# A new hand-run order for a fused cross attention and mixture-of-experts kernel: other places, PSUM banks and copying engines for the same steps

## The chip, the cores and the metric

The kernel runs on one core of one Trainium2 chip. Its engines are TensorE (PE in the profile; PEld is its loading of weights), VectorE (DVE), ScalarE (ACT), GpSimd (POOL) and SyncE (SP). The metric is device time in microseconds. The kernel before takes 209.95 us, the median of three runs from 209.51 to 209.97.

## The reference

Cross attention between 512 tokens and 32 states in each of 8 batches and 8 heads of width 64, both ways round, and then a two-layer network over all rows that come out. In float32:

```
scores  = x @ state.T / 8                       # per batch and head: 512 x 32
xread   = softmax(scores,   over the states) @ state      # 512 x 64
sread   = softmax(scores.T, over the tokens) @ x          # 32 x 64
rows    = concat(xread, sread), heads side by side        # 8 * 544 = 4352 rows of 512
h       = rows @ w_in                                     # 4352 x 2048
g       = max(h, 0) + alpha * min(h, 0)                   # alpha: one number per column
out     = g @ w_out                                       # 4352 x 512
```

Sums of softmax have 1e-9 added, which the kernel leaves out.

## The kernel before, in words

**Arithmetic.** All operands of matmuls are f16, all sums are f32. Since xread = a @ state, h of a batch is a @ (state @ w_in): the kernel makes m = state @ w_in for a batch (L486, 64-deep matmuls; it is copied from PSUM by L508), and then h for each of 16 blocks of 128 hidden columns (jc) as two 512-wide matmuls of m with the transposed attention weights aT (L519). The state reads of all batches are gathered in a tile XS (copied by L472) and go through w_in by themselves as a ninth "batch" of 256 rows (L528). g is made in two steps: ACT writes neg = relu(-h) (L551) and DVE writes gp = neg * (1 - alpha) + h (L569).

**The second layer.** Batch 0 takes plain products of gp with w_out (L588, called o, copied out by L761). Batches 1 to 7 and the reads take a scheme of seven products on 2x2 blocks instead of eight. It needs block sums of gp (s, numbered 1 to 4; L645 on POOL, or L621: a DMA from gp to gp that adds, issued by POOL) and sums of blocks of w_out (ws, L616, once). The products p (L668) add up in three PSUM chains per batch. From these, copies p1, p5 and u are taken (L699), c21 is a copy (L703), and c11, c12 and c22 are additions on DVE (L706). Each of the four c blocks is stored by SP (L579) or, near the end, by ACT (L582). For batch 7 the block c11 is made in three last pieces by L717 and L728.

**The attention of one batch.** Scores (sc, L326, 16 small matmuls) need x transposed (xT): for batches 0 and 1 by PE, for batches 2 to 7 by a DMA that transposes, issued by SP (L304), from the loaded x (xg, L175, issued by POOL, which casts to f16). For the softmax over the states DVE transposes 32x32 blocks of the scores (ts, L357) and takes maxima (mx, L365), POOL subtracts (L371), ACT takes exponentials (L377), DVE sums and inverts (L381, L382), POOL scales (an, L387), DVE transposes back (aT, L397). For the softmax over the tokens DVE takes maxima (nb, L409), ACT takes exponentials with sums (e, L424), e is scaled on ACT (L440) or POOL (L442), and a second transposing DMA on SP makes e2T (L446), from which PE makes the state reads (sr_ps, L461).

**What sets the order.** Nothing is planned by the compiler. One string, ORDER (from L17 on), lists some 1,180 tokens, and the program walks through it; each token calls one step, and the steps' instructions stand in each engine's own queue in just that order. An engine takes its next instruction only when the one before has been issued and its own waits are over. The numbers behind a token are batch, block and PSUM bank (k0 to k5 are single banks, and there is one double tile for scores and m); a letter names the engine that copies (a for ACT, v for DVE, p for POOL; d stands for the adding DMA). So `F.1.7.0` is h of batch 1, block 7, in bank 0; `N` and `G` are the neg and gp of a block; `S` and `P` are products; `A.1.1.0.d` is block sum 1 of half 0 of batch 1 by DMA; `sc`, `xd`, `tt`, `lx`, `m`, `mo`, `rd` and `rdo` are scores, transposing of x, transposing of e, load of x, m, the copy of m, the state reads and their copy; `T` is a weight sum, `Q` a block of the result, `W` a store, `Z` a number of matmuls on zeros (L245), which write to a bank that nobody reads.

**Buffers** that tie places in the list together: 2 for xT, 4 for xg, 2 for e2T, 5 for results to be stored (osb; p1, p5, u and the c blocks share them), 4 for neg, 2 for gp, 3 for each half's block sums. SP's queue holds, in one order, the six transposes of x, the eight of e and nearly all stores. POOL's queue holds the loads of x, w_in and w_out and the adding DMAs between its own sums.

Of the kernel before, what the change touches and what calls it, by code (L numbers as in the profile page):

```python
# [23 lines left out]
f.0.0.0.5 mo.0.0.a.1 xo.1.1.1.v xt.1.0.1.3 wo.2 f.0.2.0.4 tsum.0 m.1.1 wb.0.1 mo.3.0.a.0 xo.1.0.1.v
m.0.1.0.2 mo.1.1.v.0 tn.0.0 mo.0.1.v.0 f.0.2.1 f.0.0.1 mo.1.1.a.1 mo.0.1.a.1 f.0.1.0.1 f.0.1.1
F.0.3.3 m.4.0 N.0.0 N.0.1 F.0.5.2 N.0.2 F.0.4.0 G.0.0 G.0.1 N.0.3 G.0.2 F.0.7.5 N.0.5 N.0.4 G.0.3
S.0.1.0.1 mo.4.0.a.0 S.0.0.0.4 mo.4.0.a.1 G.0.4 S.0.0.1 S.0.1.1 lx.2 N.0.7 m.0.2.3.0 sc.1 G.0.5
mo.0.2.a.0 S.0.2.0.2 wo.3 G.0.7 m.1.2.5.3 mo.0.2.a.1 mo.1.2.a.0 S.0.2.1 sb.1 F.0.6.0 xd.2 mo.1.2.a.1
F.0.8.5 N.0.6 F.0.9.3 tm.1 S.0.1.2 N.0.8 S.0.2.2 S.0.0.2 G.0.6 S.0.1.3 te.1.1 te.1.0 N.0.9 F.0.11.0
smax.1 N.0.11 S.0.2.3 m.0.3 G.0.8 F.0.10.5 tn.0.1 T.0.0.p T.0.1.p S.0.0.3 mo.0.3.a.0 G.0.9 N.0.10  # L30
G.0.11 ssh.p.1 T.2.0.p S.0.3.0.3 mo.0.3.v.1 S.0.3.1 F.0.13.0 S.0.3.2 sexp.1 N.0.13 G.0.10 S.0.3.3
m.1.3 ssum.1 G.0.13 F.0.14.5 S.0.2.4 snorm.p.1 T.1.0.p N.0.14 G.0.14 S.0.1.4 wb.1 tt.0 F.0.12.0
N.0.12 G.0.12 S.0.0.4 F.0.15.5 S.0.3.4 mo.1.3.a.1 N.0.15 tsum.1 tn.1.0 S.0.1.5 G.0.15 S.0.0.5
S.0.2.5 mo.1.3.a.0 m.2.1 tn.1.1.a F.1.7.0 mo.2.1.v.0 S.0.2.6 N.1.7 mo.2.1.v.1 F.1.3.5 lx.3 tt.1
G.1.7 sc.2 S.0.2.7 tx.2 T.1.1.p F.1.9.0 O.0.2.a S.0.0.6 N.1.3 S.0.1.6 sb.2 N.1.9 S.0.0.7 ty.2
# [5 lines left out]
wb.2 W.O.0.0 P.1.1.3 N.1.15 m.2.2 N.1.13 P.1.2.1 A.1.3.1.p G.1.15 mo.2.2.a.1 F.1.14.0 mo.2.2.a.0
G.1.12 F.2.13.2 N.1.14 G.1.13 m.3.2 N.2.13 F.2.12.1 G.1.14 A.1.1.0.d mo.3.2.a.1 F.2.0.3 N.2.12
P.1.2.2 G.2.13 A.1.2.0.p F.2.9.0 N.2.0 G.2.12 P.1.2.3 N.2.9 F.2.8.2 G.2.0 Q.1.p1.a F.2.4.1
mo.3.2.a.0 tsum.2 G.2.9 A.1.1.1.d F.2.2.3 N.2.4 P.1.6.0 Q.1.c11.v W.Q.1.c11 xd.4 A.1.2.1.p tn.2.1.a
F.2.11.0 G.2.4 sc.3 N.2.11 P.1.6.1 tx.3 N.2.2 F.2.10.4 P.1.5.0.1 T.3.1.p N.2.10 G.2.11 P.1.6.2 ty.3
N.2.8 P.1.5.1 G.2.2 P.1.6.3 tn.2.0.a F.2.5.0 sb.3 Q.1.u.a tt.2 F.2.1.3 lx.5 P.1.5.2 G.2.8 P.1.7.0
te.3.0 A.1.4.0.p P.1.5.3 smax.3 te.3.1 P.1.7.1 F.2.3.2 N.2.5 G.2.10 P.1.7.2 Q.1.p5.a ssh.p.3 m.3.3
N.2.1 G.2.5 P.1.7.3 mo.3.3.a.1 G.2.1 P.1.3.0 N.2.3 F.2.15.4 tsum.3 Q.1.c22.v mo.3.3.a.0 P.1.3.1
A.1.4.1.p N.2.15 P.2.1.0.0 G.2.3 sexp.3 F.2.6.3 G.2.15 sc.4 P.1.4.0 tn.3.0.a tx.4 P.2.2.0.2
A.2.3.0.p F.2.7.4 ssum.3 P.2.2.1 ty.4 N.2.7 P.1.4.1 N.2.6 P.1.3.2 te.4.0 P.2.1.1 G.2.6 snorm.p.3  # L50
P.1.4.2 te.4.1 G.2.7 P.2.1.2 tn.3.1.a P.1.3.3 sb.4 F.2.14.3 tt.3 A.2.2.0.p P.1.4.3 N.2.14 tsum.4
P.2.1.3 Q.1.c12.v Q.1.c21.a rd.2.4 wb.3 W.Q.1.c22 Q.2.p1.a m.3.1 W.Q.1.c21 rdo.2.a m.5.1.1.5
A.2.1.0.d mo.3.1.a.0 P.2.2.2 G.2.14 xd.5 P.2.6.0 mo.5.1.a.0 A.2.3.1.p smax.4 F.3.10.4 mo.3.1.a.1
P.2.2.3 mo.5.1.a.1 F.3.13.3 N.3.10 Q.2.c11.v m.4.3 N.3.13 G.3.10 F.3.7.1 A.2.2.1.p P.2.6.1 W.Q.2.c11
N.3.7 G.3.13 F.3.2.5 mo.4.3.a.0 W.Q.1.c12 F.3.0.2 G.3.7 N.3.2 F.3.8.4 N.3.0 F.3.1.3 G.3.2 A.2.1.1.d
F.3.3.1 N.3.1 G.3.0 ssh.p.4 P.2.6.2 N.3.3 F.3.5.5 G.3.1 N.3.8 P.2.5.0.2 G.3.3 mo.4.3.a.1 P.2.6.3
N.3.5 lx.6 rd.3.3 Q.2.u.v sexp.4 m.4.2 G.3.5 A.2.4.0.p F.3.14.1 rdo.3.a G.3.8 P.2.5.1 mo.4.2.a.1
P.2.7.0 ssum.4 N.3.14 F.3.4.5 F.3.15.3 N.3.4 P.2.7.1 N.3.15 G.3.14 P.2.5.2 snorm.p.4 mo.4.2.a.0
P.2.7.2 G.3.4 P.2.5.3 G.3.15 sc.5 Q.2.p5.a m.4.1.4.1 tx.5 P.2.7.3 lx.7 mo.4.1.a.0 F.3.6.5 mo.4.1.a.1
F.3.12.3 A.2.4.1.p Q.2.c22.v N.3.6 P.2.3.0 ty.5 wb.4 N.3.12 F.3.11.1 P.2.4.0 te.5.0 F.3.9.4 G.3.6  # L60
N.3.11 P.2.3.1 A.3.3.0.p N.3.9 P.2.4.1 G.3.12 xd.6 F.4.0.5 G.3.11 P.2.4.2 N.4.0 F.4.7.3 sb.5
A.3.3.1.p P.2.4.3 N.4.7 P.3.1.0.1 Q.2.c21.a G.4.0 P.2.3.2 tn.4.0.a P.3.1.1 G.3.9 F.4.3.0 te.5.1
G.4.7 P.2.3.3 A.3.1.0.d N.4.3 P.3.1.2 tsum.5 A.3.1.1.d tn.4.1.a G.4.3 m.5.0 m.5.2.5.4 A.3.2.0.p
mo.5.0.a.0 P.3.1.3 mo.5.2.v.1 mo.5.2.a.0 F.4.1.3 Q.2.c12.v P.3.2.0.0 F.4.11.4 mo.5.0.v.1 Q.3.p1.a
W.Q.2.c12 P.3.2.1 A.3.2.1.p smax.5 N.4.1 tt.4 m.6.2 F.4.8.5 mo.6.2.a.0 P.3.6.0 G.4.1 N.4.11
W.Q.2.c22 P.3.2.2 N.4.8 G.4.11 F.4.4.2 W.Q.2.c21 mo.6.2.a.1 A.3.4.1.p F.4.5.3 G.4.8 xd.7 N.4.4
P.3.6.1 N.4.5 P.3.2.3 G.4.4 tn.5.1.a sc.6 Q.3.c11.v m.5.3.4.5 tn.5.0.p F.4.13.2 mo.5.3.a.0 tx.6
P.3.6.2 N.4.13 P.3.5.0.0 mo.5.3.a.1 P.3.6.3 G.4.13 ssh.p.5 ty.6 tt.5 P.3.5.1 Q.3.u.a sb.6 F.4.6.4
F.4.2.5 N.4.6 W.Q.3.c11 P.3.7.0 G.4.5 N.4.2 A.3.4.0.p P.3.5.2 sexp.5 P.3.7.1 G.4.2 F.4.14.2 G.4.6
P.3.5.3 N.4.14 P.3.7.2 ssum.5 Q.3.p5.a A.4.3.0.p F.4.12.3 te.6.1 F.4.15.5 P.3.3.0 G.4.14 N.4.15  # L70
F.4.10.4 G.4.15 P.3.7.3 N.4.10 snorm.p.5 P.3.3.1 Q.3.c22.v te.6.0 P.4.1.0.2 smax.6 F.4.9.5 N.4.12
P.3.3.2 N.4.9 A.4.3.1.p P.4.1.1 G.4.10 P.3.3.3 P.3.4.0 G.4.9 P.4.1.2 G.4.12 P.3.4.1 A.4.1.0.d
Q.3.c12.v m.6.3 m.6.0.4.5 A.4.2.0.p mo.6.3.a.0 rd.4.3 mo.6.0.v.0 W.Q.3.c12 mo.6.3.a.1 rd.5.0 tsum.6
wb.5 W.Q.3.c22 tn.6.1.a sc.7 P.3.4.2 mo.6.0.a.1 P.4.1.3 rdo.5.v ssh.p.6 tx.7 P.3.4.3 Q.4.p1.a
P.4.2.0.4 rdo.4.a F.5.0.5 sb.7 F.5.11.0 A.4.1.1.d N.5.0 P.4.6.0 N.5.11 A.4.2.1.p P.4.2.1 G.5.0
Q.3.c21.a P.4.6.1 G.5.11 sexp.6 P.4.2.2 F.5.8.3 smax.7 F.5.2.5 P.4.2.3 N.5.2 F.5.9.1 ssh.p.7
Q.4.c11.v tn.6.0.a F.5.1.0 G.5.2 ty.7 P.4.6.2 W.Q.4.c11 N.5.9 P.4.5.0.4 N.5.1 W.Q.3.c21 G.5.9
P.4.6.3 A.4.4.0.p N.5.8 F.5.3.5 tt.6 G.5.1 Q.4.u.a P.4.5.1 te.7.1 ssum.6 F.5.14.1 P.4.7.0 N.5.14
F.5.5.0 A.4.4.1.p N.5.3 P.4.5.2 G.5.14 te.7.0 P.4.7.1 G.5.8 P.4.5.3 N.5.5 F.5.7.1 tsum.7 G.5.3
P.4.7.2 snorm.p.6 N.5.7 G.5.5 m.6.1 Q.4.p5.a m.7.3.3.5 G.5.7 P.4.7.3 mo.7.3.a.1 P.4.3.0 mo.7.3.v.0  # L80
A.5.3.0.p F.5.15.0 Q.4.c22.v F.5.6.1 N.5.15 P.4.3.1 wb.6 N.5.6 W.Q.4.c22 F.5.10.3 P.4.4.0 N.5.10
G.5.6 P.4.3.2 F.5.12.5 G.5.10 P.4.3.3 N.5.12 F.5.4.1 A.5.1.0.d Q.4.c12.v mo.6.1.a.0 P.4.4.1 tn.7.0.p
G.5.15 F.6.14.3 P.4.4.2 mo.6.1.v.1 N.5.4 F.6.10.4 G.5.12 N.6.14 P.5.1.0.0 tn.7.1.p P.4.4.3 N.6.10
G.5.4 P.5.1.1 sexp.7 G.6.10 F.6.0.5 A.5.2.0.p F.6.12.1 tt.7 G.6.14 N.6.0 P.5.1.2 Q.4.c21.a G.6.0
F.5.13.4 F.6.5.3 W.Q.4.c21 N.5.13 P.5.2.0.2 W.Q.4.c12 N.6.12 A.5.3.1.p G.5.13 P.5.1.3 P.5.2.1 G.6.12
Q.5.p1.a m.7.2 N.6.5 m.7.0.5.4 ssum.7 P.5.2.2 mo.7.0.a.1 P.5.6.0 mo.7.0.a.0 A.5.2.1.p F.6.3.1 G.6.5
P.5.2.3 N.6.3 F.6.2.4 Q.5.c11.v F.6.4.5 N.6.2 G.6.3 F.6.13.3 W.Q.5.c11 A.5.1.1.d N.6.4 P.5.6.1
mo.7.2.v.1 N.6.13 A.5.4.1.p F.6.15.2 G.6.4 P.5.5.0.1 N.6.15 P.5.6.2 G.6.2 F.6.1.5 G.6.15 P.5.6.3
# [744 lines left out]
```

## Time and profile before

| | |
|---|---|
| median of three runs | 209.95 us |
| span of the profiled execution | 208.5 us |
| PE busy | 200.2 us, 96% |
| POOL busy | 180.9 us, 87% |
| DVE busy | 175.2 us, 84% |
| ACT busy | 145.5 us, 70% |
| moved by DMA | 27.11 MB, mean 130 GB/s |

The span is that of one execution taken by the hardware profiler, from the first to the last instruction; it is 1.45 us below the median of the timed runs. Each row of a timeline or of the chain gives a start in us, a length in us, the engine, the line of the kernel and what was written from what; "x4" is a count of instructions. An arrow in brackets names what ended an idle time. SPq and ACTq mark DMA issues; the time from an issue to its landing is listed apart. Line numbers are those of the kernel before; in the changed kernel all lines behind the list stand 10 lower.

### The profile page before, as it was taken

The numbers are of one execution on the slowest core, as the hardware profiler recorded it, in microseconds if no ns is written. First come the engines' busy times: TensorE is split into PE (matmuls) and PEld (weight loads), VectorE is DVE, ScalarE is ACT, GpSimd is POOL, SyncE is SP. The second block draws the span as 40 slices with busy tenths as digits, with TensorE's granted clock in tenths as the row PEclk, the third lists the DMA queues.
The fourth block names the chain that finished last, engine by engine and source line by source line (L and its number), as shares of the span: only waits on it lengthen the run. The fifth ranks groups of instructions, "written<-read, shape, count | busy, mean of one in ns | idle before, by whom it ended". The sixth has DMA issues, their size and how long they took to land.

```text
span 208.5 us, 5136 instructions
## 1 busy us (share of the span) xinstructions
PE 200.2 (96%) x2034; PEld 135.3 (65%) x2034; DVE 175.2 (84%) x273; ACT 145.5 (70%) x291; POOL 180.9 (87%) x119
## 2 busy tenths in 40 slices
...
PEclk9999999999999999999999999999999999999999
...
GB/s 148 177 204 208 205 203 149 103 132 191 218 144 142 116 58 212 206 126 165 183 225 100 43 146 166 24 82 151 104 0 53 23 78 154 37 63 156 50 153 104
DMA packets 44793, 27.11 MB, mean 130 GB/s; under 512 B 22097, under 2 KB 42465, under 8 KB 44769
## 3 DMA queue, kind: packets, MB, share of 16 engines
q0 software_dynamic: 14192, 12.03, 38.5%
...
q8 instruction: 16, 0.26, 0.5%
...
## 4 chain that ended last, share of the span: by engine, by line
PE 70%; DVE 14%; ACT 5%; DMA 4%; POOL 3%; issue 2%; DVEq 0%; POOLq 0%
PE p L668 41%; PE h L519 18%; DVE gp L569 8%; DMA w_in_sb<-in_moe_w_in_dram 4%; PE h L528 3%; PE m_ps L486 3%; PE sr_ps L461 2%; ACT m L508 1%; DVE aT L397 1%; ACT neg L551 1%; DVE m L508 1%; POOL s L645 1%; ACT e L424 1%; POOL an L387 1%; PE o L588 1%
## 5 line engine op out<-in xcount | busy, mean ns | idle before, releaser
L551 ACT ACTIVATE neg<-h 128x512 f32<-128x512 f32 (+1 forms) x144 | 78.5, 583 | 27.4 <-PE h L519 18.5
L569 DVE SCALAR_TENSOR_TENSOR gp<-neg,oma_sb,h 128x512 f16<-128x512 f32 x128 | 89.0, 735 | 6.7 <-ACT neg L551 6.4
L519 PE MATMUL h<-aT,m 128*128 128x512 f16 x250 | 68.6, 379 | 0.3 <-DVE gp L569 0.3
L645 POOL TENSOR_TENSOR s<-gp,s 128x1024 f16<-128x1024 f16 x28 | 65.7, 2393 | 1.2 <-DVE gp L569 0.6
L668 PEld LDWEIGHTS <-gp 128*128 128x128 f16 x432 | 41.7, 98 | 13.9 <-issue 1.9
L668 PEld LDWEIGHTS <-s 128*128 128x128 f16 x368 | 35.2, 98 | 12.7 <-POOL s L645 1.7
L668 PE MATMUL p<-ws,s 128*128 128x256 f16 x248 | 37.3, 273 | 0.2 <-POOL s L645 0.2
L645 POOL TENSOR_TENSOR s<-gp 128x1024 f16<-128x1024 f16 x14 | 31.6, 2260 | 6.5 <-DVE gp L569 6.4
L519 PEld LDWEIGHTS <-m 128*128 128x128 f16 x250 | 23.6, 98 | 16.1 <-issue 3.3
L668 PE MATMUL p<-ws,gp 128*128 128x256 f16 x224 | 33.6, 273 | 0.0
L508 ACT CAST m<-m_ps 128x512 f16<-128x512 f32 x51 | 28.8, 600 | 4.8 <-PE m_ps L486 3.6
L668 PE MATMUL p<-w_out_sb,gp 128*128 128x256 f16 x208 | 30.6, 273 | 0.0
L371 POOL TENSOR_TENSOR ts<-ts,mx 128x1024 f32<-128x1024 f32 (+1 forms) x9 | 17.1, 1905 | 6.0 <-DVE mx L365 6.0
L668 PE MATMUL p<-w_out_sb,s 128*128 128x256 f16 x120 | 18.3, 273 | 0.0
L387 POOL TENSOR_TENSOR an<-ts,r 128x1024 f16<-128x1024 f32 (+1 forms) x9 | 16.3, 1808 | 1.8 <-DVE r L382 1.8
L588 PE MATMUL o<-w_out_sb,gp 128*128 128x512 f16 x64 | 16.6, 380 | 0.1
L621 POOL DMA_DIRECT2D gp<-gp x14 | 13.2, 962 | 3.4 <-issue 2.9
L569 DVE SCALAR_TENSOR_TENSOR gs<-neg,oma_sb,h 128x256 f16<-128x256 f32 x16 | 7.2, 478 | 8.2 <-ACT neg L551 8.2
L486 PE MATMUL m_ps<-w_in_sb,stT 64*32 64x512 f16 x256 | 11.7, 383 | 0.3 <-DMA w_in_sb<-in_moe_w_in_dram 0.2
L588 PEld LDWEIGHTS <-gp 128*128 128x128 f16 x64 | 5.9, 98 | 8.1 <-issue 1.3
L424 ACT ACTIVATE e<-sc,nb 128x512 f16<-128x512 f32 x16 | 11.0, 693 | 0.1
L699 ACT COPY p<-p 128x512 f32<-128x512 f32 x11 | 6.5, 588 | 6.4 <-PE p L668 6.4
...
## 6 DMA issues: line engine op xcount, KB each, us to landing
out_dram<-c SPq DMA_DIRECT2D x27, 256.0 KB, 3.1
xg<-in_x_dram POOLq DMA_DIRECT2D x7, 512.0 KB, 8.7
gp<-gp POOLq DMA_DIRECT2D x14, 256.0 KB, 3.6
w_in_sb<-in_moe_w_in_dram POOLq DMA_DIRECT2D x4, 512.0 KB, 11.8
w_out_sb<-in_moe_w_out_dram POOLq DMA_DIRECT2D x4, 512.0 KB, 13.1
out_dram<-osb SPq DMA_DIRECT2D x4, 256.0 KB, 3.0
...
x<-in_x_dram SPq DMA_DIRECT2D x1, 256.0 KB, 3.2
```

The lines of the kernel that those rows point to most:

```text
L371: engine(e).tensor_tensor(ts, ts, over_blocks(cols(live["mx", b], j, S // N)), ALU.subtract)
L387: engine(e).tensor_tensor(blocks(cols(live["an", b], j, S)), blocks(cols(live["ts", b], j, S)), over_blocks(cols(live["r1", b], j, S // N) ...
L424: nc.scalar.activation(live["e2", b][:, g, :, :], live["sc", b][:, :, :, g, :].rearrange("p r j s -> p (r j) s"), EXP, bias=live["nb", b][ ...
L486: nc.tensor.matmul(t[N * k : N * (k + 1), :], st_head(b, h)[64 * r : 64 * r + 64, :], w_in_sb[64 * r : 64 * r + 64, c, 512 * f : 512 * (f ...
L508: copier(e)(m_tile(b)[:, f, g, :], live["mp", b, f][g])
L519: nc.tensor.matmul(h.rearrange("p (r j s) -> p r j s", r=2, j=2), ms[b][:, f, g, 128 * j : 128 * (j + 1)], weights(b, g), start=(g == 0), ...
L551: nc.scalar.activation(neg, h, RELU, bias=0.0, scale=-1.0)
L569: nc.vector.scalar_tensor_tensor(gt, negs.pop((b, jc)), oma_sb[:, jc : jc + 1], h, ALU.mult, ALU.add)
L588: nc.tensor.matmul(outs[b, q], token_cols(b, jc, q), w_out_sb[:, jc, :], start=(jc == 0), stop=(jc == n_jc - 1),)
L621: nc.gpsimd.dma_start(gp[:, 1, 0], gp[:, 1, 1], accum_op=ALU.add)
L645: engine(e).tensor_tensor(t, x, y, op)
L668: nc.tensor.matmul(chains[chain][:, t, :], lhs, rhs[:, i, :], start=(opens and i == 0 and t == 0), stop=(i == half_k - 1), skip_group_chec ...
```

## The change

The list ORDER is replaced by another with nearly the same tokens (1,178 before, 1,175 now). One step gets an argument for its engine:

```diff
 ORDER = """
-lx0 id lst stc xc.1.v xc.0.a oma wi.0 lx.1 Z.1.20 stt.0 Z.2.9 xt.0.1.0.1 xt.0.0.0.2 xo.0.1.0.v
...
-    def first_states_cast():
+    def first_states_cast(e):
         live["st0"] = consts.tile([128, 2, D], F16, name="st0")
-        nc.vector.tensor_copy(live["st0"], st0_32)
+        copier(e)(live["st0"], st0_32)
```

The counts of what the two lists issue differ in little: 90 zero matmuls instead of 82; 58 of the 64 copies of m on ACT instead of 51, and 6 on DVE instead of 13; of eight copies of xT two on ACT instead of one; both first casts of x on ACT, where one was on DVE; the copy of the first transposed states on DVE, not ACT; of the eight copies of XS six on ACT instead of five; seven scalings of e on POOL instead of six, and nine on ACT instead of ten; the subtraction for batch 6 on DVE, not POOL; of 24 copies p1, p5 and u 17 on ACT, as before, though others. Of the block sums 50 are on POOL and 14 are adding DMAs, in both. All 14 transposing DMAs are on SP, in both. What differs most is the order of the steps and the PSUM bank of each. Three places follow.

The first is PE's queue ahead of the scores of batch 2 (sc_2). h_1_7 is h of batch 1, block 7, o_0_2 the product of batch 0 for its third group of tokens, gp_0_1 the second half of batch 0's gp. Before:

```order
L519 MATMUL h_1_7_702<-aT_1_662,m_1_318 128x512 [waits DVE_49]
...
L588 MATMUL o_0_2_527<-w_out_sb_82,gp_0_1_488 128x512 [waits DMASW3_49]
...
L519 MATMUL h_1_3_711<-aT_1_662,m_1_318 128x512 [waits DVE_49]
...
L326 LDWEIGHTS stT_87 [waits DMAHW4_49,DVE_49]
L326 MATMUL sc_2_720<-xT_2_553,stT_87 32x2x128 [waits PE_49]
```

and now:

```order
L578 MATMUL o_0_3_685<-w_out_sb_82,gp_0_0_445 128x512 [waits DVE_49]
...
L578 MATMUL o_0_1_484<-w_out_sb_82,gp_0_1_473 128x512 [waits DMASW3_49]
...
L316 LDWEIGHTS stT_87 [waits DMAHW4_49,PE_49]
L316 MATMUL sc_2_697<-xT_2_678,stT_87 32x2x128 [waits Activation_49]
...
L509 LDWEIGHTS m_1_352 [waits DVE_49]
L509 MATMUL h_1_7_733<-aT_1_731,m_1_352 128x512 [waits PE_49]
L509 LDWEIGHTS m_1_352
L509 MATMUL h_1_0_743<-aT_1_731,m_1_352 128x512
```

The first blocks of h of batch 1 stood ahead of the scores of batch 2 and stand behind them now.

The second is SP's queue between 59 and 77 us of the profile before. c11_1 is a result of batch 1, osb_0_2 one of batch 0; xT_4 is the transposed x of batch 4, e2T_2 the transposed e of batch 2. Before:

```order
L579 DMA out_0_dram<-osb_0_0_765 128x512 [waits DMAHW3_49]
L579 DMA out_0_dram<-c11_1_1068 256x1x256 [waits DMAHW4_49,DVE_49]
L304 DMA_TRANSPOSE xT_4_1071<-xg_4_901 128x16x128 [waits DMAHW5_49,DMASW5_49,PE_49]
L446 DMA_TRANSPOSE e2T_2_1145<-e2_2_778 128x8x128 [waits DMAHW6_49,PE_49,Activation_49]
L446 DMA_TRANSPOSE e2T_3_1324<-e2_3_1161 128x8x128 [waits DMAHW7_49,PE_49,Activation_49]
```

and now:

```order
L569 DMA out_0_dram<-osb_0_3_840 128x512 [waits DMAHW2_49,Activation_49]
L436 DMA_TRANSPOSE e2T_2_1060<-e2_2_760 128x8x128 [waits DMAHW3_49,DMAHW5_49,PE_49,Activation_49]
L569 DMA out_0_dram<-osb_0_2_798 128x512 [waits DMAHW4_49]
L294 DMA_TRANSPOSE xT_4_1212<-xg_4_934 128x16x128 [waits DMASW6_49]
L569 DMA out_0_dram<-c11_1_1068 256x1x256 [waits DMAHW6_49,DVE_49]
L436 DMA_TRANSPOSE e2T_3_1312<-e2_3_1142 128x8x128 [waits DMAHW7_49,PE_49,Activation_49]
```

The transposing of e of batch 2 and one store have moved ahead of that of x of batch 4.

The third is SP's queue between 83 and 105 us, where c11_2, c22_2, c12_2 are results of batch 2. Before:

```order
L579 DMA out_0_dram<-c12_1_1339 256x1x256 [waits DMAHW4_49]
L304 DMA_TRANSPOSE xT_6_1705<-xg_6_1516 128x16x128 [waits DMAHW5_49,DMASW3_49,PE_49]
L579 DMA out_0_dram<-c12_2_1803 256x1x256 [waits DMAHW6_49,DVE_49]
L446 DMA_TRANSPOSE e2T_4_1826<-e2_4_1292 128x8x128 [waits DMAHW7_49,PE_49,Activation_49]
L579 DMA out_0_dram<-c22_2_1663 256x1x256 [waits DMAHW0_49]
L579 DMA out_0_dram<-c21_2_1737 256x1x256 [waits DMAHW1_49]
L304 DMA_TRANSPOSE xT_7_1868<-xg_7_1651 128x16x128 [waits DMAHW2_49,DMASW4_49,PE_49]
```

and now:

```order
L569 DMA out_0_dram<-c11_2_1435 256x1x256 [waits DMAHW4_49,DVE_49]
L294 DMA_TRANSPOSE xT_7_1704<-xg_7_1684 128x16x128 [waits DMAHW5_49,DMASW3_49,PE_49]
L294 DMA_TRANSPOSE xT_6_1723<-xg_6_1702 128x16x128 [waits DMAHW1_49,DMAHW6_49,DMASW4_49,PE_49]
L569 DMA out_0_dram<-c22_2_1674 256x1x256 [waits DMAHW7_49,DVE_49]
L569 DMA out_0_dram<-c12_2_1757 256x1x256 [waits DMAHW0_49,DVE_49]
```

Batch 7's x is transposed ahead of batch 6's, and both ahead of the stores of c22 and c12 of batch 2. On POOL the load of x of batch 7 likewise comes ahead of batch 6's. The load of x of batch 3 comes ahead of batch 1's normalising (an) on POOL, where it came behind it, and that of batch 4 comes behind the first adding DMA of batch 1, where it came ahead of it.

More of the change, by code (lines that the diff above doesn't have):

```diff
@@ L24 @@
[L24 to L35, printed above, removed]
@@ L41 @@
[L41 to L52, printed above, removed]
@@ L53 @@
[L53 to L88, printed above, removed]
@@ new lines @@
+N.2.14 N.2.7 te.4.0 G.2.7 sb.4 P.2.1.0.5 P.2.1.1 W.Q.1.c11 N.2.15 G.2.15 T.3.1.p P.1.4.2 P.1.4.3 Q.1.c21.a
+tn.3.1.a tt.3 W.Q.1.c21 P.1.3.2 P.2.1.2 P.1.3.3 Q.1.c12.v m.3.1 mo.3.1.a.0 mo.3.1.a.1 rd.2.1 m.5.1.3.4
+mo.5.1.a.0 mo.5.1.a.1 P.2.1.3 rdo.2.a tsum.4 tn.4.0.a A.2.3.0.p P.2.2.0.2 P.2.2.1 A.2.1.0.d snorm.p.3 wb.3
+G.2.14 P.2.2.2 F.3.13.4 N.3.13 smax.4 G.3.13 F.3.11.0 N.3.11 G.3.11 Q.2.p1.a P.2.2.3 Q.2.c11.v m.4.3 xd.5
+W.Q.1.c22 F.3.8.1 F.3.3.4 mo.4.3.a.1 N.3.3 G.3.3 F.3.0.3 N.3.8 G.3.8 F.3.5.0 N.3.5 F.3.4.2 G.3.5 A.2.2.0.p
```

118 lines of the change are left out of this document (82 added, 36 removed).

## The prediction

> **What bounds the kernel now.** I read the page first, then the chain that ended last, then what PE waited for, then busy time by stretch.
>
> ```profile
> span 208.5 us, 5136 instructions
> PE 200.2 (96%) x2034; PEld 135.3 (65%) x2034; DVE 175.2 (84%) x273; ACT 145.5 (70%) x291; POOL 180.9 (87%) x119
> PEclk9999999999999999999999999999999999999999
> ```
>
> PE is busy for 96% of the span, and its clock is full in every slice, so no clock is to be won or lost. POOL, DVE and ACT have 27 to 63 us to spare over the whole, but the average hides stages, so the chain comes next (start, length, what):
>
> ```profile
> 38.65 1.21 DVE m L508 x2
> 53.80 4.59 DVE gp L569 x7
> 58.44 1.20 POOL gp L621
> 59.64 2.17 POOL s L645
> 61.86 1.48 PE p L668 x12
> 71.63 3.06 PE p L668 x28
> 80.75 2.16 PE h L519 x10
> ...
> 117.29 0.56 PE m_ps L486 x16
> 117.85 1.12 PE sr_ps L461 x64
> ```
>
> Up to 61.86 us the chain changes engines: DVE, then a block sum on POOL that the products of batch 1 need. From 61.86 us on it is PE nearly alone. The view of PE's waits from 62 to 205 us has one row, and the table by stretch says how full PE is on both sides:
>
> ```profile
> PE p L668 <- POOL s L645: 0.2, 1, 0.2
> ...
> 39.90:61.86 21.96, 21.75 (x227) 11.50 (x227) 21.93 (x31) 20.71 (x45) 21.91 (x14) 1.00 0.94 159
> 61.86:204.89 143.03, 142.97 (x1434) 105.35 (x1434) 121.23 (x184) 95.84 (x194) 127.76 (x75) 1.00 0.57 112
> ```
>
> (The columns are the length, then PE, PEld, DVE, ACT and POOL busy with counts, clock, DMA share, GB/s.) After 61.86 us PE waits 0.2 us in 143. Before it, from the scores of batch 2 at 39.90 us on, all four engines are full, and the DMA engines at 0.94. So the time is made of three things: when PE reaches that product (the third piece of product 6, batch 1), what PE stalls afterwards, and the tail.
>
> **What PE has to do does not change.** From that product on, both orders give PE the same 209 groups of products, 103 of h, 17 of m, 4 of scores, 6 of state reads and the last pieces. Nothing can be won there but the 0.2 us. A stall on the other hand is paid whole.
>
> **The change part by part.**
>
> *Arrival at product 6 of batch 1.* Between the scores of batch 2 and that product the new order has 25 groups of h and 10 of o, where there were 23 and 8. A group is two 512-wide matmuls: 10 in 2.16 us above, so 0.216 us each; 8 more are 1.73 us. They stood ahead of the scores before. So PE reaches the scores 1.73 us earlier, if nothing stops it, and needs 1.73 us more behind them. What could stop it are the scores' inputs:
>
> ```profile
> 39.90 0.41 PE L326 MATMUL sc<-xT,stT 64*32 64x256 f16 x16
> 39.90 0.14 PEld L326 LDWEIGHTS <-stT 64*32 64x32 f16 x16 [0.57 <-DVE m L508]
> ...
> 32.29 3.17 SPq L304 DMA_TRANSPOSE xT<-xg  x1
> 35.51 5.42 SPq L446 DMA_TRANSPOSE e2T<-e  x2
> ```
> ```profile
> xg<-in_x_dram POOLq DMA_DIRECT2D x1, 512.0 KB, 13.0
> w_out_sb<-in_moe_w_out_dram POOLq DMA_DIRECT2D x1, 512.0 KB, 15.7
> ```
> ```profile
> xT<-xg SPq DMA_TRANSPOSE x1, 6.0
> ...
> xT<-xg SPq DMA_TRANSPOSE x1, 4.7
> ```
>
> Before, the scores waited 0.57 us for the copies of m on DVE (38.65 us in the chain). The transposed x of batch 2 was there already: issued at 32.29, landed 6.0 us later, at 38.3. That issue waits for the load of x, which is in flight for 13.0 us among the weight loads; the new order leaves it as the ninth load of that queue, so 32.3 stays. PE on the other hand would be there at 39.90 - 1.73 = 38.2, or 37.6 without the 0.57. The DMA therefore decides now: 38.3. From there PE had 31 groups of h and o (0.432 each), 11 of products (4 matmuls at 0.109, 0.437), 3 of m (8 matmuls, 0.28), 2 of scores (0.41) and 2 of state reads (32 matmuls, 0.56): 13.39 + 4.80 + 0.84 + 0.82 + 1.12 = 21.0 us. Now it has 22.74. The stretch took 21.96, so 0.96 us of it PE did not fill: 38.3 + 22.74 + 0.96 = 62.0, against 61.86: **+0.15**. Bounds: without the 0.96, 61.04 (-0.8); with the slowest landing of such a transfer (6.9, below) and a start that a load beside it delays by half a us, 63.4 (+1.5). I take the value of the same transfer, 6.0.
>
> POOL, which decided here, loses one scaling of e in this stretch:
>
> ```profile
> 38.10 1.56 POOL L442 TENSOR_SCALAR e<-e,r 128x512 f16<-128x512 f16 x1
> ```
>
> The sum was ready at 61.81, so it is ready at about 60.3 now and falls out of the path.
>
> *Scores of batch 4.* Behind the product, 9 groups of products, 4 of h and one of m stand ahead of these scores, 5.94 us by the same rates; before it were 12, 5 and 1, 7.68 us. So PE is there at 62.0 + 5.9 = 67.9. The transposed x of batch 4 stood ahead of batch 2's e in SP's queue and stands behind it now, and behind a store. That e waits for its scaling on ACT, 40 ACT instructions after the first copy of o (at about 39.4). In the stretch above ACT ran 45 in 21.96 us, 0.49 each: 39.4 + 40 x 0.49 = 59. SP's times from the timeline (issuing durations, then flight times):
>
> ```profile
> 46.34 0.84 SPq L579 DMA_DIRECT2D out_dram<-osb  x2
> 47.60 2.07 SPq L304 DMA_TRANSPOSE xT<-xg  x1
> ...
> 60.48 4.09 SPq L304 DMA_TRANSPOSE xT<-xg  x1
> ...
> 93.46 3.10 SPq L304 DMA_TRANSPOSE xT<-xg  x1
> ```
> ```profile
> xT<-xg SPq DMA_TRANSPOSE x1, 6.9
> ...
> xT<-xg SPq DMA_TRANSPOSE x1, 6.1
> ```
>
> Issue of e takes 2.7 (half of 5.42), of the store 0.4 to 0.8: x of batch 4 goes out at about 62.4. It lands 4.7 (93.46, few loads beside it) to 6.9 us later (47.60, an x load beside it): 67.1 to 69.3. With 6.1, the row of this same transfer at 60.48, 68.5: a wait of 0.6; POOL's load of that x is issued behind an accumulating DMA now, some 4 us later than before, which can only delay. **+0.7**, bounds 0 and +1.6.
>
> *SP around 90 to 106 us.* The transposing of x of batch 7 comes ahead of batch 6's, and both stand ahead of the store of c22 of batch 2. The load of x of batch 6 waits for batch 3's state reads, which by PE's work come at about 90 us; x loads fly 8.7 us in the median:
>
> ```profile
> xg<-in_x_dram POOLq DMA_DIRECT2D x7, 512.0 KB, 8.7
> out_dram<-c SPq DMA_DIRECT2D x27, 256.0 KB, 3.1
> ```
>
> So it lands at 98.7 or later, its transposing takes SP 3.1, the store is out at about 102 and landed 3.1 later, at 105. The sum c11 of batch 3 on DVE reuses that store's buffer, and is due at about 104.9. Wait 0 to 1.5 on DVE, of which PE sees what exceeds DVE's lead: **+0.2**.
>
> *PSUM banks.* By PE's own work about 12 banks are opened again within 1.3 us of their last reader, against 8; before, that gave no wait in the list above. 0 to +0.6, **+0.2**.
>
> *Copying engines.*
>
> ```profile
> L508 ACT CAST m<-m_ps 128x512 f16<-128x512 f32 x51 | 28.8, 600 | 4.8 <-PE m_ps L486 3.6
> L371 POOL TENSOR_TENSOR ts<-ts,mx 128x1024 f32<-128x1024 f32 (+1 forms) x9 | 17.1, 1905 | 6.0 <-DVE mx L365 6.0
> L245 PE MATMUL z<-zero 128*128 128x128 f16 x82 | 7.6, 249 | 1.7 <-DVE zero L239 1.1 <-ACT m L508 0.4 <-DVE xT L317 0.2
> ```
>
> Seven copies of m go from DVE to ACT: 7 x 28.8/51 = 4 us more on ACT, about as much less on DVE; one copy of the first states and the casts of x trade places. One subtraction of about 1.9 us (batch 6) goes from POOL to DVE, one scaling of e from ACT to POOL. All of it lies beside PE, whose 143 us cover ACT's 96 and POOL's 128 in the last stretch. If that cover were thin anywhere, it would be ahead of 61.86 us, where ACT is at 20.7 of 22. Eight zero matmuls more (7.6/82 = 0.09 us each, 0.7 us) stand in waits of the start for loads: 0. Fifty sums on POOL and 14 by DMA stay as they are: 0.
>
> *Tail.*
>
> ```profile
> 204.51 0.38 PE L668 MATMUL p<-ws,gs 128*128 128x256 f16 x2
> 204.72 0.28 DVE L728 TENSOR_TENSOR osb<-p,o 128x128 f32<-128x128 f32 x1
> 204.83 1.20 SPq L579 DMA_DIRECT2D out_dram<-c  x2
> 205.03 0.38 ACTq L582 DMA_DIRECT2D out_dram<-osb  x1
> ```
>
> From PE's end at 204.89 it takes 3.6 us to the end of the span, for the last copies and stores. In the new order the last piece comes last on PE and the copy of c21 about 0.5 us earlier: **-0.2**, bounds -0.4 and 0.
>
> Sum: 0.15 + 0.7 + 0.2 + 0.2 - 0.2 = +1.05 on a span of 208.5. The median of the runs, 209.95, is 1.45 above the span: 209.55 + 1.45 = **211.0**.
>
> **A rule against this.** The Trainium skill, "DMA: Bandwidth & Descriptors", section "Latency and other measured facts", gives a DMA transpose an effective 261 GB/s; 512 KB would be an estimate of 2.0 us, where the rows show 4.7 to 6.9, so the trace disagrees. By that figure x of batch 2 would land at 34.3 and of batch 4 at 64.4, neither would stop PE, and the sum would be that of the first rival.
>
> **The rivals.**
>
> *Faster: transposes kept apart land early.* The row at 93.46 landed in 4.7. If x of batch 2 does, at 37.0, PE comes to the scores at 37.6, and with the lighter DVE half or all of the 0.96 goes: 37.6 + 22.74 + 0 to 0.96 = 60.3 to 61.3, 0.6 to 1.5 ahead; batch 4 then lands at 67.1 and costs 0 to 0.8. With the tail: 208.4 to 209.4, say 208.9. For it speaks that the 0.57 wait at 39.90 is one for DVE, which is relieved. Against it, that the load of x of batch 3 moves ahead of POOL's normalising of batch 1 (to about 33 us), into the flight of just this transposing. It decides from a flight below 5.3 us. The same page's section "Queues, rings and completion order" says that a DMA engine takes turns between its queues by packet; the 6.9 with a load beside it and the 4.7 agree, and it speaks against this rival.
>
> *No change.* Batch 2 lands as before (+0.15), batch 4's wait falls in its lower bound (0), banks and c11 give none, tail -0.2: 209.9, with +-0.6. The shared 143 us speak for it.
>
> *Much slower: SP's queue blocks.* One transposing that waits holds every store behind it, each store holds an output buffer, and so DVE, then PSUM, then PE. Upper bounds: 1.5 + 1.6 + 1.5 + 0.6 - 0.2 = +5.0, 215; with half of them 212.5. For it: the two transposes ahead of c22. Against it: five output buffers and DVE's 22 us to spare in the last 143.
>
> **How the numbers follow.** The forecast (210.6 to 212) 0.42, faster 0.25, no change 0.18, much slower 0.15. About 0.3% (0.63 us) is what a measurement of this kernel can tell from no change. Of the forecast's share a little reaches below 210.58: faster 0.26, same 0.20, slower 0.54. The range leaves out a quarter of the faster rival and the upper half of the slow one: 208.7 to 213.3. The likeliest's own range is 210.4 to 212.
>
> **What would show it.** Right: the scores of batch 2 start at 38.2 to 38.5 and wait for the DMA of x; product 6's third piece starts at about 62.0 with no wait for POOL; the scores of batch 4 wait 0 to 1.6 us for their DMA; PE's waits after 62 us add to about 1. Wrong: scores of batch 2 before 37.8 or after 39.2; waits on POOL's sums, which I have at none; a wait of PE above 1 us anywhere after 70 us for ACT or DVE.

## The result and the profile after

The changed kernel takes 219.19 us, the median of five runs from 217.18 to 222.95, against 209.95: 1.042 times the time before, with a 95% interval of 1.038 to 1.047. The forecast was 211.0, with a range of 208.7 to 213.3: the sign was right, the size was not. The runs of the changed kernel scatter by 6 us, those of the kernel before by 0.5 to 2 us; the profile is of the fastest run, 217.18. Ratios, here and below, leave out runs that took over 1.5% longer than the fastest of the same kernel.

From its page, to be set against the lines of before:

```profile
span 215.0 us, 5156 instructions
PE 201.5 (94%) x2042; PEld 137.3 (64%) x2042; DVE 174.3 (81%) x265; ACT 148.8 (69%) x299; POOL 181.6 (84%) x119
PEclk9999999999999999999987999999999999999999
```

The work is the same to a few us on every engine, and the span is 6.5 us longer. New is a dip of the granted clock in the middle. The view of what PE waited for (in us in total, times, longest), its three largest rows:

```profile
PE m_ps L476 <- DVE c L696: 3.0, 1, 3.0
PE sc L316 <- DMA xT<-xg: 2.4, 1, 2.4
PE h L509 <- DVE gp L559: 1.5, 1, 1.5
```

The timeline shows the second of these, and then how DVE comes to the first:

```profile
41.01 0.41 PE L316 MATMUL sc<-xT,stT 64*32 64x256 f16 x16 [2.40 <-DMA xT<-xg]
```
```profile
32.87 3.44 SPq L294 DMA_TRANSPOSE xT<-xg  x1
...
97.07 6.17 SPq L294 DMA_TRANSPOSE xT<-xg  x2
103.33 3.02 SPq L569 DMA_DIRECT2D out_dram<-c  x2
```
```profile
xT<-xg SPq DMA_TRANSPOSE x1, 8.0
...
out_dram<-c SPq DMA_DIRECT2D x1, 256.0 KB, 8.0
```
```profile
111.48 0.69 DVE L696 TENSOR_TENSOR c<-p,p 128x512 f32<-128x512 f32 x1 [3.53 <-DMA out_dram<-c]
```

The transposed x of batch 2 flew 8.0 us instead of 6.0, and its scores started at 41.01, 1.1 later than before. At 97 us the two transposes of x went out, at 103.33 the store of c22 of batch 2, and that too flew 8.0 us. DVE stood until 111.5 for the buffer, and PE behind DVE for a bank. The table by stretch shows what that cost (length, then PE, PEld, DVE, ACT, POOL busy with counts, clock, DMA share, GB/s):

```profile
41.01:63.58 22.57, 22.57 (x228) 12.00 (x229) 21.69 (x30) 21.23 (x44) 19.51 (x13) 1.00 0.74 130
63.58:109.20 45.62, 45.62 (x466) 30.72 (x465) 43.34 (x61) 40.75 (x85) 44.93 (x27) 1.00 0.93 148
109.20:112.22 3.02, 0.07 (x9) 0.00 (x0) 0.74 (x2) 1.17 (x2) 3.02 (x2) 0.92 1.15 281
112.22:115.10 2.88, 2.88 (x33) 1.69 (x33) 2.88 (x4) 0.00 (x0) 2.19 (x2) 0.50 0.65 209
115.10:211.68 96.58, 96.58 (x944) 74.70 (x942) 73.57 (x115) 55.08 (x113) 79.61 (x47) 1.00 0.33 83
```

Product 6 of batch 1 was reached at 63.58, 1.7 later than before. PE then stood for 3.0 us and came back at half the clock, which held for 2.9 us and cost about 1.4 more. The sum of 1.7 + 3.0 + 1.4 is 6.1 of the span's 6.5. The tail was 0.3 shorter, 3.3 us, so some 0.7 us is not accounted for, and the time outside the span 2.2 us in every run, where the profile of before had 1.45 and its other runs 1.8.

This accounts for one run, and the fastest. What the others had on top, the experiments show.

### The profile page after: what moved, and what is told of

Its sections match the earlier page's. It is cut to its first block, busy times and chain, and to the rows that moved or that the text cites. A ratio compares the mean times of both kernels' runs of the same rounds, so it can differ in the third digit from the quotient of the medians.

```text
span 215.0 us, 5156 instructions
## 1 busy us (share of the span) xinstructions
PE 201.5 (94%) x2042; PEld 137.3 (64%) x2042; DVE 174.3 (81%) x265; ACT 148.8 (69%) x299; POOL 181.6 (84%) x119
## 4 chain that ended last, share of the span: by engine, by line
PE 78%; DMA 13%; DVE 5%; issue 1%; POOL 1%; ACT 1%; DVEq 0%; POOLq 0%
PE p L658 40%; PE h L509 22%; DMA xg<-in_x_dram 5%; PE o L578 4%; DMA out_dram<-c 4%; DMA xT<-xg 4%; PE m_ps L476 3%; PE h L518 3%; PE sr_ps L451 2%; DVE gp L559 2%; PE sc L316 1%; PE o L707 1%; DVE nb L403 1%; PE h L530 1%; DVE c L696 1%
## 5 line engine op out<-in xcount | busy, mean ns | idle before, releaser
L509 PE MATMUL h<-aT,m 128*128 128x512 f16 x250 | 66.5, 380 | 1.5 <-DVE gp L559 1.5
L635 POOL TENSOR_TENSOR s<-gp,s 128x1024 f16<-128x1024 f16 x28 | 64.2, 2398 | 0.4
L658 PEld LDWEIGHTS <-gp 128*128 128x128 f16 x432 | 41.8, 98 | 12.9 <-issue 1.3
L635 POOL TENSOR_TENSOR s<-gp 128x1024 f16<-128x1024 f16 x14 | 32.1, 2326 | 2.7 <-DVE gp L559 2.6
L498 ACT CAST m<-m_ps 128x512 f16<-128x512 f32 x58 | 32.5, 607 | 1.9 <-PE m_ps L476 1.7
L658 PE MATMUL p<-ws,s 128*128 128x256 f16 x248 | 33.5, 277 | 0.0
L658 PE MATMUL p<-ws,gp 128*128 128x256 f16 x224 | 29.6, 273 | 0.0
L658 PE MATMUL p<-w_out_sb,gp 128*128 128x256 f16 x208 | 27.6, 273 | 0.0
L361 POOL TENSOR_TENSOR ts<-ts,mx 128x1024 f32<-128x1024 f32 (+1 forms) x8 | 15.1, 1885 | 7.1 <-DVE mx L355 7.1
L693 ACT COPY c<-p 128x512 f32<-128x512 f32 (+1 forms) x7 | 4.0, 565 | 12.4 <-PE p L658 12.4
L696 DVE TENSOR_TENSOR c<-p,p 128x512 f32<-128x512 f32 x13 | 8.9, 683 | 4.0 <-DMA out_dram<-c 3.5
L432 POOL TENSOR_SCALAR e<-e,r 128x512 f16<-128x512 f16 x7 | 12.0, 1719 | 0.0
```

The lines of the kernel that those rows point to most:

```text
L361: engine(e).tensor_tensor(ts, ts, over_blocks(cols(live["mx", b], j, S // N)), ALU.subtract)
L432: engine(e).tensor_scalar_mul(e2, e2, r2)
L498: copier(e)(m_tile(b)[:, f, g, :], live["mp", b, f][g])
L509: nc.tensor.matmul(h.rearrange("p (r j s) -> p r j s", r=2, j=2), ms[b][:, f, g, 128 * j : 128 * (j + 1)], weights(b, g), start=(g == 0), ...
L635: engine(e).tensor_tensor(t, x, y, op)
L658: nc.tensor.matmul(chains[chain][:, t, :], lhs, rhs[:, i, :], start=(opens and i == 0 and t == 0), stop=(i == half_k - 1), skip_group_chec ...
```

## The experiments

Times are in us, the kernel before taking 209.9 to 210.0 beside each. The ratio is to that time; for the second and the fifth there is none.

| | median, lowest to highest | ratio and interval | flight of batch 2's x | subtraction of batch 6 |
|---|---|---|---|---|
| changed kernel | 219.19, 217.18 to 222.95 | 1.042, 1.038 to 1.047 | 8.0 | DVE 1.71 |
| 1 store first | 220.49, 218.17 to 227.22 | 1.039, 1.036 to 1.042 | 8.2 | DVE 5.25 |
| 2 load late | 216.56, 212.34 to 220.29 | - | 5.1 | DVE 2.94 |
| 3 both | 215.37, 214.84 to 217.10 | 1.028, 1.023 to 1.033 | 5.0 | DVE 5.42 |
| 4 zeros in the wait | 219.43, 215.69 to 221.46 | 1.034, 1.025 to 1.043 | 8.7 | DVE 2.53 |
| 5 three undone | 212.77, 210.15 to 217.25 | - | 5.8 | POOL |
| 6 before, subtraction on DVE | 216.00, 214.64 to 218.44 | 1.026, 1.019 to 1.033 | 5.6 | DVE 5.05 |
| 7 six buffers | 220.22, 217.71 to 223.89 | 1.039, 1.031 to 1.046 | 9.5 | DVE 5.20 |
| 8 before, load early | 210.94, 209.95 to 215.00 | 1.004, 1.001 to 1.007 | 8.5 | POOL |
| 9 as 6, zeros in the wait | 213.74, 213.67 to 214.78 | 1.019, 1.016 to 1.021 | 5.5 | DVE 5.06 |
| 10 subtraction on POOL | 214.78, 212.15 to 218.13 | 1.013, 1.009 to 1.017 | 7.2 | POOL |
| 11 subtraction and load | 212.47, 211.09 to 212.70 | 1.010, 1.007 to 1.013 | 4.6 | POOL |
| 12 three undone, spread | 212.48, 210.56 to 216.96 | 1.009, 1.005 to 1.012 | 5.4 | POOL |

**1. The store ahead of the transposes.** One token moves:

```diff
 lx.6
+W.Q.2.c22
 xd.7
...
-W.Q.2.c22
 F.4.4.2
```

> The changed kernel with one store moved: that of c22 of batch 2 goes ahead of the two transposes of x in SP's queue. Theory (the queue): the block was ready at about 92 us and sat behind the transposes until 103.33, so DVE's wait of 3.5 us at 108 us, PE's wait of 3.0 us and the half clock for 2.9 us behind it all go: 4.4 us less, about 214.5 us, clock 1.00. Rival (traffic): the store is late because it flies among transposes and adding DMAs; then the next store or transpose takes over the delay, PE waits 1 to 3 us somewhere between 95 and 125 us, and the time stays above 217.

220.49 us: nothing gained. Yet the wait that it was to remove is gone, and PE's list of waits from 60 us on has one row, another:

```profile
PE p L658 <- DVE gp L559: 3.5, 1, 3.5
```

What DVE did at that time, and POOL beside it (start, length, a count of instructions):

```profile
116.04 5.25 DVE L361 TENSOR_TENSOR ts<-ts,mx 128x1024 f32<-128x1024 f32 x1
```
```profile
113.72 2.32 POOL L377 TENSOR_TENSOR an<-ts,r 128x1024 f16<-128x1024 f32 x1
115.59 4.61 POOL L635 TENSOR_TENSOR s<-gp 128x1024 f16<-128x1024 f16 x2
```

One instruction of DVE, the subtraction for batch 6 that the change moved from POOL to DVE, takes 5.25 us. In the changed kernel's own profile it took 1.71. It ends at 121.29, 1.1 us after POOL's two block sums, which end at 120.20. So both theories missed the new wait. The queue theory was right on the place, but what PE gained there it lost 10 us further on. The rival's time, above 217, came true, but not by its traffic.

**2. The load of x of batch 3 later.**

```diff
-lx.3 xd.3
 snorm.p.1 wb.1 F.1.7.3 T.1.1.p
+lx.3 xd.3
 T.1.0.p
```

> The changed kernel with the load of x of batch 3 issued some 5 us later, behind the normalising of batch 1 and one weight sum. Theory (the load collides with the transposing of batch 2's x): that flight falls from 8.0 us to about 6.0, the scores of batch 2 start at 39.0 instead of 41.01, and 1.5 to 2 us are gained: 217 to 217.7 us. Rival (the transposing is slowed by the weight loads and the transposes of e behind it): the flight stays at 7.5 to 8 us and the time at 219.

The load is issued at 37.84 instead of 34.01, and the flight is 5.1 us: PE's wait for the DMA ahead of the scores of batch 2 is gone. The median falls by 2.6 us, to 216.56, but the four runs lie between 212.34 and 220.29, so the size is uncertain; the mechanism is confirmed by the flight, and by the eighth experiment. In the profiled run, the fastest (212.34), the wait for the store of c22 was down to 1.6 us and the clock stayed at 1.00.

**3. Both edits.**

> Both edits. If the two losses are independent, 219.2 - 4.4 - 1.8 = 213 us, with the span near 210.5. If the lost time has one common cause, or a later wait takes its place, 215 or more.

215.37: "a later wait takes its place" was the right half. The subtraction takes 5.42 us, and PE waits 3.7 us behind it:

```profile
113.09 5.42 DVE L361 TENSOR_TENSOR ts<-ts,mx 128x1024 f32<-128x1024 f32 x1
```
```profile
112.70 4.72 POOL L635 TENSOR_TENSOR s<-gp 128x1024 f16<-128x1024 f16 x2
```

Again DVE ends (118.51) 1.1 us after POOL (117.42).

**4. Zeros in the wait.** To tell a clock that falls because PE idles from one that falls for another reason:

```diff
+Z.2.32
 m.5.3.1.2
```

> The changed kernel with 32 matmuls on zeros (about 2.9 us at full clock) ahead of the m matmuls that wait for DVE at 109 us; the wait itself stays. Theory (the clock falls because PE idles): PE is busy through the wait, the clock stays at 1.00 behind it, and 1.4 us are gained: 217.7 us. Rival (the clock is cut for another reason, as the load of the last 100 us): the clock falls to 0.5 at the same place all the same, and the time stays at 219 or rises by what the zeros cost.

The median, 219.43, tells nothing within this scatter, and the profiled run could not decide the question. PE had stood 4.1 us at the scores of batch 2 for the transposed x and came to the place of the zeros later. There DVE had only 0.5 us left to wait for the store, so the zeros stood in no long wait.

```profile
111.35 0.69 DVE L696 TENSOR_TENSOR c<-p,p 128x512 f32<-128x512 f32 x1 [0.46 <-DMA out_dram<-c]
```
```profile
38.00:42.20 4.20, 0.20 (x1) 0.00 (x0) 0.61 (x1) 0.38 (x1) 4.12 (x3) 1.00 1.35 156
42.20:46.00 3.80, 3.72 (x25) 1.49 (x26) 2.47 (x3) 1.78 (x3) 0.70 (x1) 0.58 0.75 174
...
112.10:114.05 1.95, 1.95 (x42) 1.80 (x34) 1.20 (x2) 1.22 (x2) 1.95 (x2) 1.00 0.80 177
114.05:118.00 3.95, 3.95 (x52) 2.88 (x51) 3.14 (x3) 1.07 (x2) 3.34 (x2) 1.00 0.46 144
```

Behind the idle time at 38 us the clock is 0.58 over 3.8 us. That it is 1.00 behind the zeros proves nothing here, since PE had no long wait to fill. The test that decides came with the ninth experiment.

**5. Three undone: the subtraction on POOL as well.** On top of the third:

```diff
-ssh.v.6
+ssh.p.6
```

> The changed kernel with three things undone: the load of x of batch 3 later, the store of c22 of batch 2 ahead of the transposes, and the subtraction for batch 6 back on POOL. Theory (with the store moved, DVE reaches its subtraction while POOL makes two block sums, and cannot run it until they end: 5.42 us instead of 1.71, and PE waits 3.7 us for it): that wait of PE and the lower clock behind it go, 4 to 5 us less than with two undone: 210.5 to 211.5 us, clock 1.00. Rival (PE's wait at 116 us is that of a DVE which is late by all its work, not by this one instruction): with the same work less 1.7 us on DVE and 1.9 us more on POOL, the sums are later and PE still waits 2 us or more: 213 to 215.

212.77, but two of the four runs took 210.15 and 210.55, with the clock at 1.00, and two took 215 and 217. In the profiled run (210.55) the longest wait of PE after 60 us is 0.6. Those two are at the theory's lower end, 210.5, or just below it; what stops PE in the other two no profile caught.

**6. The kernel before, with the subtraction on DVE alone.** The same token the other way round, in the order of before.

> The kernel before with this one part of the change alone: the subtraction for batch 6 on DVE. Theory (DVE and POOL exclude each other): the instruction takes 2 to 6 us on DVE or lengthens a sum on POOL by as much, PE waits for DVE 1 to 4 us near 125 to 130 us: 211 to 215 us. Rival (only its 1.2 to 1.9 us of work move, beside PE): 210.0 within 0.3.

216.00: 6.0 us slower by one token, above what the theory had at most. DVE and POOL:

```profile
119.03 5.05 DVE L371 TENSOR_TENSOR ts<-ts,mx 128x1024 f32<-128x1024 f32 x1
```
```profile
117.62 2.38 POOL L645 TENSOR_TENSOR s<-gp,s 128x1024 f16<-128x1024 f16 x1
119.70 1.13 POOL L621 DMA_DIRECT2D gp<-gp  x1
120.31 2.68 POOL L645 TENSOR_TENSOR s<-gp,s 128x1024 f16<-128x1024 f16 x1
```

and what came of it on PE:

```profile
123.29:127.06 3.77, 0.01 (x2) 0.00 (x1) 3.77 (x5) 1.06 (x1) 0.00 (x0) 0.89 0.01 2
127.06:132.98 5.92, 5.92 (x22) 3.27 (x22) 5.51 (x7) 2.98 (x6) 4.11 (x3) 0.50 0.36 105
```

DVE ends at 124.08, 1.1 us after POOL's second sum. PE idles for 3.8 us and then works at half the clock for 5.9, which is 3 us more. The rival, that the work only moves beside PE, is refuted, and with it the step of the prediction.

**7. Six result buffers instead of five,** with the order left alone:

```diff
-    st = consts.tile([128, n_j, D], F16)
+    st = att.tile([128, n_j, D], F16, name="st", tag="e2T", bufs=2)
...
-        osb = moe.tile(shape, F32, name=f"{name}_{b}", tag="osb", bufs=5)
+        osb = moe.tile(shape, F32, name=f"{name}_{b}", tag="osb", bufs=6)
```

(and likewise wherever osb stands)

> The changed kernel with six result buffers instead of five (the loaded states share memory with e2T to make room); the order stays. Theory (c11 of batch 3 waits only for the buffer of the stuck store): DVE's wait of 3.5 us and PE's of 3.0 us at 109 us go. By the port theory DVE then meets POOL's sums at its subtraction as in the first experiment, and PE waits 3 to 4 us there: 217 to 220 us. Rival (no such collision, so the whole 4.4 us come back): 214.8.

220.22. DVE waits for no store any more, so the buffer was what held it; and the subtraction, now met at the wrong moment, takes 5.20 us and PE waits 3.5 for it, as the port theory had it. The two stalls hide each other. In three profiles of this order and its variants DVE was held up by the store: 3.5 us in the changed kernel, 2.2 in the second experiment, 0.5 in the fourth. There the subtraction took 1.71, 2.94 and 2.53 us. In the three in which no store held it up (1, 3 and 7) it took 5.20 to 5.42. Why the delay lets it in earlier, the traces don't show.

**8. The kernel before, with the load of x of batch 3 early.**

```diff
+lx.3
 snorm.p.1
...
-lx.3
 tt.1
```

> The kernel before with one part of the change alone: the load of x of batch 3 ahead of batch 1's normalising on POOL. Theory (it collides with the transposing of batch 2's x): that flight goes from 6.0 to 7.5 to 8 us, the scores of batch 2 start at 40 to 40.5 instead of 39.9, and 0.3 to 1.0 us are lost: 210.3 to 211. Rival (the flight has no more to do with this load): 6.0, and 210.0.

The flight of batch 2's x is 8.5 us instead of 6.0, PE waits 1.7 us for it, and the kernel takes 1.004 times as long, 0.1 to 0.7%: 0.8 us, as the theory had it. Over all runs, the flight is 7.2 to 9.5 us with the load early (six kernels) and 4.6 to 6.0 with it late (eight, before among them).

**9. As the sixth, with zeros in PE's wait.**

```diff
+Z.1.60
 F.5.2.5
```

> The kernel before with the subtraction for batch 6 on DVE, as in the sixth experiment (216.0), and 60 matmuls on zeros (3.6 us) put where PE waited 3.8 us for DVE. Theory (half of the loss is the clock, which falls because PE idles): DVE's 5 us stay, PE's real work is as late, but the clock stays at 1.00: 2 to 2.5 us less, 213.5 to 214. Rival (the clock falls for another reason): 0.5 behind the place again, 216.

213.74, all four runs within 1.1 us, against 216.00: 2.3 us come back though PE's real work is as late as there. DVE still takes 5.06 us. The clock behind the zeros is 1.00:

```profile
125.00:127.00 2.00, 2.00 (x40) 2.00 (x38) 2.00 (x3) 1.06 (x1) 0.00 (x0) 1.00 0.02 3
127.00:129.00 2.00, 1.59 (x24) 1.27 (x22) 2.00 (x3) 0.00 (x0) 0.00 (x0) 1.00 0.00 0
129.00:131.00 2.00, 1.95 (x14) 1.17 (x12) 2.00 (x4) 1.70 (x5) 0.57 (x1) 1.00 0.04 8
```

So of what the subtraction costs the kernel before, some 2 us are the clock alone (2.3 of 6.0 by the medians, 1.5 of 5.5 by the ratios), and it fell because PE idled.

**10. The changed kernel with only the subtraction undone.**

> The changed kernel with the subtraction for batch 6 back on POOL and nothing else. Theory (each of three places can stop PE by itself): the wait for the store of c22 at 109 us (3 us, and the clock behind it) and that for the transposed x of batch 2 (2.4 to 4) are still there; where the changed kernel's run had the first, its subtraction cost nothing: 217 to 219. Rival (the subtraction is the cause of all): 211 to 213.

214.78, between the two: 4.4 us less than the changed kernel, by the subtraction alone, and still 1.013 times the time before. The two runs that this ratio counts took 212.15, within the rival's range, and 213.53, just above it; the profile is of a longer one, 216.03. In it the waits for batch 2's x (2.1 us) and at the store of c22 (1.6 us) are there, as the theory had it, and the clock is at 0.50 behind the first of them:

```profile
40.29 0.41 PE L316 MATMUL sc<-xT,stT 64*32 64x256 f16 x16 [2.06 <-DMA xT<-xg]
```
```profile
42.00:43.00 1.00, 1.00 (x4) 0.30 (x2) 1.00 (x1) 0.63 (x2) 0.94 (x1) 0.50 1.29 260
43.00:44.00 1.00, 1.00 (x4) 0.35 (x3) 0.55 (x2) 0.80 (x2) 0.00 (x0) 0.50 1.04 300
```

The subtraction is the largest cause, and not all.

**11. Subtraction and load undone, the store left behind the transposes.**

> The changed kernel with the subtraction back on POOL and the load of x of batch 3 late; the store of c22 stays behind the two transposes. Theory: only the wait for that store is left; PE comes earlier to it than in the changed kernel, so DVE waits 2 to 5 us and PE 1.5 to 4: 212 to 216. Rival (the store would not hold anybody up without the other two): 210.5, as with all three undone.

212.47, and the four runs are within 1.6 us. The number lies in the theory's range. In the profiled run, the fastest (211.09), DVE waited for the store, but only 0.5 us, and PE had no wait for it:

```profile
DVE c L696 <- DMA out_dram<-c: 0.5, 1, 0.5
```

The transposes were out 2 us sooner here (95.14), so the store went at 101.26, and it flew 4.8 us instead of 8.0. In this run the rival is right: the store's place in the queue cost PE nothing. What the other three runs, some 1.4 us longer, waited for, no profile shows.

**12. Three undone, and the second transposing behind another store.**

```diff
-xd.6
...
 W.Q.2.c12
+xd.6
```

> As with three things undone (212.8, scattering from 210.2 to 217.3), and the transposing of batch 6's x also put behind the store of c12 of batch 2, so that SP holds no store behind two transposes. Theory (what scatters is SP's queue at 94 to 104 us): the runs come to 210 to 211 and scatter by less than 1.5 us. Rival (the scatter is from elsewhere, such as the flight of batch 2's x): still 210 to 217.

212.48, from 210.56 to 216.96: no better than the fifth or the eleventh. Two of the six runs still took 216 and 217, so stores that stand behind two transposes are not what scatters. The edit also brought a wait of its own: in the profiled run (211.98) the scores of batch 6 stood 1.5 us for the transposed x that had been put later.

**Where the time went.** By the ratios the changed kernel is 8.9 us above the kernel before. With the subtraction back on POOL it is 2.8 above (10), with the load of batch 3 later as well 2.1 (11). So the subtraction is worth 6.1 us, about as much as alone in the kernel before, and by the medians 4.4. The load is worth 0.7 here by the ratios and 2.3 by the medians, 0.8 alone (8) and 2.5 between the first and the third experiment; its size stays uncertain. The profile of the changed kernel does not show the subtraction's price, because in that run the stall at the store came in its place. That each of the other runs of this order lost time at one of the two places fits experiments 1, 3 and 7, but is not shown. Of the remaining 2.1 us the profile of 11 shows 0.65, a wait of PE for a copy of m on DVE at 136.8 us, which before did not have; the time outside the span is 0.2 above before's. The rest stays open, as does what disturbs some runs of 5 and 12. The wait at the store of c22 was PE's longest in the profile of the changed kernel, and moving the store, or giving DVE a buffer more, gained nothing. No version tried here beats the kernel before.

## Why the prediction was wrong, point by point

The sign came out right, but hardly by the terms that stood for it: of the +1.05, 0.7 did not come at all, and most of what did come stood in the sum at 0 to 0.2. Two of the prediction's own signs of being wrong appeared: the scores of batch 2 started after 39.2, at 41.01, and PE waited 3.0 us for DVE after 70 us.

**"The DMA therefore decides now" (scores of batch 2): right in mechanism, short in size.** The scores waited for the transposed x. I took the flight of before, 6.0, and held 6.9 for the slowest; with the load beside it, it was 8.0, and up to 9.5 in other runs. The load moving "into the flight of just this transposing" was named, as an argument against the faster rival; it belonged in the sum. Product 6 came at 63.6 instead of 62.0: +1.7 for +0.15, just above the bound of 1.5. The error in the landing was larger, 2.6 us (40.9 for 38.3). It was partly made up by luck: from the scores on PE took 22.57 us where 22.74 + 0.96 had been reckoned. The 0.96 was called time that PE did not fill, but the row of before has PE busy in 21.75 of the 21.96 us; where it came from, and why it went, stays open.

**"All of it lies beside PE, whose 143 us cover ACT's 96 and POOL's 128": this step failed.** The subtraction was priced as 1.9 us of work that changes engines. The price is not in its work: DVE cannot run it while POOL makes a block sum, and POOL's block sums fill nearly half of the span (64.2 and 32.1 us in their two largest groups on the page of the changed kernel). It took 1.7 to 5.4 us on DVE, ended 1.1 us after POOL's last sum in five profiles, and cost 5.5 to 6.0 us alone and 4.4 to 6.1 within the change. Totals by stretch cannot show such a thing, since they count the time of an engine as its own. The Trainium skill, "SBUF — State Buffer", section "Who interferes with whom", has the rule: a DVE instruction with two SBUF inputs contends with a GpSimd instruction that reads SBUF, and the contention is an exclusive lock. The trace agrees, with 5.05 us in the sixth experiment. It is a rule against this change, and I had not weighed it. What should have led there is that the kernel before has no two-input instruction on DVE with both operands in SBUF: each of its two-input instructions there has an operand in PSUM (L569, L706, L728), and all others stand on POOL.

**"No clock is to be won or lost": failed.** A full clock in the profile of a kernel that never idles says nothing of one that does. Behind idle stretches of 2.95 us and of 3.5 to 4.1 us the clock came back at 0.50 and stayed there for 3 to 6 us. Shorter ones do not sort by their length: behind 2.4 and 2.7 us (the changed kernel, the first experiment) it was 1.00, behind 2.06 us (the tenth) it was 0.50 for some 3 us. The Trainium skill's "TensorE: Matmul & The Clock Gate", Part 1, gives half the clock after an idle window of about 3.4 us that runs freely. The half agrees; but 2.95 us was enough here once and 2.06 us once, so the measurement decides.

**Scores of batch 4, +0.7: not seen.** The transposing went out at 65.53, 3 us later than worked out, and flew 4.6 us, about the lower bound. It landed at 70.1 and PE came at 70.5, late itself, so it did not wait, by a narrow margin.

**SP around 90 to 106 us, +0.2: right in place, wrong in price.** The store went out at 103.33 (I had 102). It landed 8.0 us later, not 3.1: a transposing was in flight with it, and two adding DMAs. DVE waited 3.5 us where I had 0 to 1.5. I had a median for a flight in the one place where the change had packed four transfers.

**PSUM banks, +0.2:** no wait of that kind by itself; the bank only passed DVE's wait to PE. **Tail, -0.2:** -0.3. **Time outside the span:** taken as 1.45, it was 2.2.

**The rivals.** The faster one fell with the flights: with the load beside it no transposing of batch 2's x came in under 7.2 us. The much slower one had the chain of the profiled run's stall step by step, from the store behind the transposes over DVE and PSUM to PE, but not that DVE and POOL exclude each other, nor the clock. Its "DVE's 22 us to spare in the last 143" were no help, because PE's next products needed the very blocks behind the stuck instruction.

**The Trainium skill's rate for transposes** ("DMA: Bandwidth & Descriptors", section "Latency and other measured facts"), weighed in the prediction, gives an estimate of 2.0 us for this transfer; it flew 4.6 to 9.5 us here, so the measurement decides again. What the Trainium skill says on the same page, in "Queues, rings and completion order", of turns between queues fits 4.6 to 6.0 without that load and 7.2 to 9.5 with it; that turns are the reason, no run here shows.
